# Late up-projections by a seven-product (Strassen-Winograd) scheme, weights' parts streamed from memory, in a kernel of windowed attention and two feed-forward nets

## The chip, the cores and the metric

The kernel runs on one core of a Trainium2 chip, in one launch. The metric is the device time in microseconds (us). The times below are of three runs and of one profiled execution.

## The reference

There are 4 sequences of 576 tokens (2304 tokens in all), 8 heads of 64, and a model width of 512. The weights arrive as 64-bit floats, q, k and v as 32-bit floats.

```python
scores = q @ k.T / sqrt(64) + alibi_bias        # causal, window of 128
x = softmax(scores) @ v                         # (2304, 512)
x = ((x @ w_a) * (x @ w_b)) @ w_out             # w_a, w_b (512, 1536), w_out (1536, 512)
h = x @ w_in                                    # (512, 2048)
g = where(h >= 1, h, where(h <= -1, 0, (h + 1) ** 2 / 4))
return g @ w_out2                               # (2048, 512)
```

## The kernel before, in words

Every matrix product of the two nets is made of three TensorE products, since each operand is kept as a rounded high part and the remainder as a low part: high by high, high by low, low by high. A weight matrix is cut into chunks of 128 hidden units: 12 chunks `a`, 12 `b` and 12 `o` for the first net, 16 `i` and 16 `p` for the second. `decode` turns one chunk of 64-bit words into its two parts, with operations on VectorE (DVE), ScalarE (ACT) and GpSimd (POOL), and `wp` holds 15 such pairs at a time.

An up-projection of one chunk (`up_steps`, lines 540 to 542) is 4 pieces of the model width by 3 products, 12 matmuls, into one PSUM bank of `mm`. In the first net `gate` multiplies the results of an `a` and a `b` chunk; in the second, `bend` applies the piecewise function. `parts` splits the result into `gh` and `gl` (line 562 and the helper `minus`, line 147, through which all such splits go). The down-projection of the chunk is another 12 matmuls, into the `acc` banks (`down1_half` line 613, `down1` lines 641 to 643, `down2` lines 679 to 681).

While the attention goes on, six half blocks of 256 tokens are passed through the first 4 or 5 chunks of the first net; their products stand between the attention's on TensorE. I call the stretch in which the attention and these half blocks are worked off the early part, and everything behind it the late part. There the tokens are taken in blocks of 512, 512, 512, 512 and 256. The hidden chunks are taken in groups (0 to 4, 4 or 5 to 8, 9 to 11 in the first net, 5, 6 and 5 chunks in the second); a group goes over all five blocks before the next begins, and so its weights stay. Between groups the sums of a block are kept in `xsum` or `osum`, and the new ones are added by VectorE. In the late part `mm` has four banks and `acc` four.

Each engine works off its own instructions in a fixed order, and so does the queue of SyncE (SP), which issues nearly all transfers. A scheduler wrote these orders when the program was built.

Of the kernel before, what the change touches and what calls it, by code (L numbers as in the profile page):

```python
# [9 lines left out]
F32 = mybir.dt.float32  # L10
# [16 lines left out]
def attention_and_two_ffns(  # L27
# [29 lines left out]
    blocks = [(t, min(TB, NT - t)) for t in range(0, NT, TB)]  # L57
# [3 lines left out]
    DEC = ['VVPP', 'VVPP', 'VVPP', 'AVPP', 'AVPP', 'AVPP', 'AVPP', 'AVPP', 'AVPP', 'AVPP', 'AVPP', 'AVPP', 'AVPP', 'AVPP', 'AVPP']  # L61
    DEC_LATER = 'AVVV'
    EB = 2
    EB2 = 2
# [6 lines left out]
    G2 = [5, 11]  # L71
# [8 lines left out]
    N0 = [4, 5, 5, 5, 5]  # L80
    N1 = 9
    NDIAG = 2
    NHALF = 6
    PACE = [0.8, 0.8, 0.5, 0.5, 0.5, 0.5, 0.5, 0.5, 0.3]
# [3 lines left out]
    TURN1 = [0, 1, 2, 3, 4]  # L88
    TURN2 = [4, 0, 1, 2, 3]
    UB = 1  # L90
    UB2 = 1
    VT = 3
    W2 = 2
    WARM = 0
    WB = 2
    WB2 = 2
    WP = 15
    HP = lambda n: n < HPN
    groups2 = [range(0, G2[0]), range(G2[0], G2[1]), range(G2[1], NF2)]
# [15 lines left out]
    if WARM:  # L115
        ps = ps_mm.tile([P, TB], F32, tag="mm", name="warm")
        for _ in range(WARM):
            nc.tensor.transpose(ps[:, :P], ident, ident)
# [21 lines left out]
    def x_tiles(i):  # L140
        n = blocks[i][1]
        return tuple(xp.tile([P, NC, n], F32R, tag=f"x{z}{i}", name=f"x{z}{i}") for z in "hl")

    xs = [x_tiles(i) for i in range(len(blocks))]
# [59 lines left out]
    def load_start():  # L204
        n = 0
        for nm in "qkv":
            start[nm] = []
            for i in range(NKB):
                start[nm].append(
                    wp.tile([P, H, D], F32, tag=f"w{'hl'[n % 2]}", name=f"{nm}{i}")  # L210
                )
                n += 1
            if TAIL < P:
                nc.gpsimd.memset(start[nm][-1][TAIL:], 0.0)
        if n % 2:
            wp.tile([P, H, D], F32, tag="wl", name="none")
        for z in range((n + 1) // 2):
            slots[0][2].append(("first", z))
# [145 lines left out]
    def values(b, hp, part):  # L364
# [31 lines left out]
        for z in range(2):  # L396
            mine = [m for m in ms if z < len(qblocks(m))]
            tok = lambda m: b * S + (2 * m + z) * D
            for i in sorted({tok(m) // TB for m in mine}):
                those = [m for m in mine if tok(m) // TB == i]  # L400
                c, n0 = (those[0] - ms[0]) * D, (tok(those[0]) - blocks[i][0]) // D
                src = po[z][:, c : c + len(those) * D].rearrange("p (n t) -> p n t", t=D)
                xh, xl = (
                    x[:, hp].rearrange("p (n t) -> p n t", t=D)[:, n0 : n0 + 2 * len(those) - 1 : 2]
                    for x in xs[i]
# [49 lines left out]
    order = [(z, f) for f in range(NF1) for z in "abo"] + [(z, f) for f in range(NF2) for z in "ip"]  # L455
    waiting = deque(order)
    wt = {}
    retired = {None}
    slots = [(wp, WP, deque())]
# [8 lines left out]
    def decode(key, pool):  # L468

        src = source(key)
        pool_, bw, be, bu = (later["dec"], WB2, EB2, UB2) if later else (wdec, WB, EB, UB)
        raw = pool_.tile([P, 4 * P], I64, tag="w64", name="w64", bufs=bw)
# [5 lines left out]
        wh = pool.tile([P, 4 * P], F32R, tag="wh", name="wh")  # L481
        wl = pool.tile([P, 4 * P], F32R, tag="wl", name="wl")
        e = pool_.tile([P, 4 * P], U32, tag="e", name="e", bufs=be)
        n = order.index(key)
        absolute, mult, add, less = DEC[n] if n < len(DEC) else DEC_LATER
        up = pool_.tile([P, 4 * P], U32, tag="up", name="up", bufs=bu)
        low = e.bitcast(F32)
        if absolute == "A":
            nc.scalar.activation(e.bitcast(F32), hi.bitcast(F32), AF.Abs)  # L489
        else:  # L490
            nc.vector.tensor_scalar(e, hi, 0x7FFFFFFF, None, ALU.bitwise_and)
        nc.vector.tensor_scalar(
            e.bitcast(F32), e.bitcast(F32), W64_MIN, W64_MAX, ALU.max, ALU.min
        )
# [15 lines left out]
    def pump():  # L510
        if not waiting:
            return False
# [291 lines left out]
```

## Time and profile before

| | |
|---|---|
| median of three runs | 996.48 us (995.35 to 998.64) |
| span of the profiled execution, first to last instruction | 994.4 us |
| TensorE (PE) busy | 969.7 us, 98% |
| weight loads (PEld) busy | 842.4 us, 85% |
| VectorE busy | 609.7 us, 61% |
| ScalarE busy | 407.2 us, 41% |
| GpSimd busy | 177.7 us, 18% |
| moved by DMA | 61.8 MB, mean 62 GB/s |

The profiled execution is 2.1 us shorter than the median of the runs, by its span. A TensorE instruction counts as busy until its result has come out of the array, and successive matmuls overlap; a busy share of 98% therefore doesn't say that the array takes a column in each cycle. How fast it goes is read from how many matmuls of one shape start in a stretch.

### The profile page before, as it was taken

Reading aid. Unit: us, or ns where it says so; the run is one execution under the profiler, and the core shown is the slowest. Engines: PE = TensorE matmul, PEld = TensorE weight load, DVE = VectorE, ACT = ScalarE, POOL = GpSimd, SP = SyncE. Lnnn points to the kernel's source line nnn. Section 1 sums busy time; section 2 is a strip of 40 time slices with the busy share of each in tenths; the row PEclk is TensorE's granted clock in tenths of the full one; section 3 lists DMA queues with packets and bytes.
Section 4 is the critical chain, followed back from the end, with each engine's and each line's share of the span. In section 5 each row is a group of like instructions: output and inputs, shape, how many; then the busy total and the mean of one; then the engine's idle time right before and its main releaser. Section 6 shows DMA issues by size and latency. Waiting matters only on the chain.

```text
span 994.4 us, 15931 instructions
## 1 busy us (share of the span) xinstructions
PE 969.7 (98%) x6052; PEld 842.4 (85%) x6052; DVE 609.7 (61%) x1366; ACT 407.2 (41%) x998; POOL 177.7 (18%) x285
## 2 busy tenths in 40 slices
PE   5997999999999999999999999999999999999998
PEld 4876999999989888888988888888888888888887
DVE  6699855553616993223995299635995446644443
ACT  5887677663214441112342245333552223322222
POOL 5567633331101100000212224000020000000001
PEclk9999999999999999999999999999999999999999
DMA  9756444213311331000331023100230000001111
GB/s 208 146 122 147 110 87 74 57 35 133 113 53 45 125 106 43 0 1 1 105 91 60 1 63 85 44 1 1 85 107 22 1 1 21 1 1 43 43 43 63
DMA packets 115403, 61.83 MB, mean 62 GB/s; under 512 B 87040, under 2 KB 107520, under 8 KB 114944
## 3 DMA queue, kind: packets, MB, share of 16 engines
q1 hardware_dynamic: 113184, 60.31, 22.7%
q8 instruction: 47, 0.77, 0.3%
q10 hardware_dynamic: 2144, 0.52, 0.2%
q14 instruction: 28, 0.23, 0.1%
HBM read 52.95 MB, written 7.86 MB: 61 GB/s over the span
## 4 chain that ended last, share of the span: by engine, by line
PE 87%; DVE 3%; DMA 1%; issue 1%; ACT 0%; POOL 0%; DVEq 0%; POOLq 0%; SPq 0%; ACTq 0%
PE mm L540 16%; PE mm L541 16%; PE mm L542 16%; PE acc L681 7%; PE acc L679 7%; PE acc L680 7%; PE acc L613 4%; PE acc L643 3%; PE acc L642 3%; PE acc L641 3%; PE ps_s L327 3%; PE ps_o L391 2%; PE ps_t L359 1%; DMA w<-in_moe_w_out_dram 1%; DVE e L499 0%
## 5 line engine op out<-in xcount | busy, mean ns | idle before, releaser
L540 PE MATMUL mm<-xh,wh 128*128 128x512 f32 (+1 forms) x912 | 318.6, 350 | 0.0
L541 PE MATMUL mm<-xl,wh 128*128 128x512 f32 (+1 forms) x912 | 315.6, 346 | 0.0
L542 PE MATMUL mm<-xh,wl 128*128 128x512 f32 (+1 forms) x912 | 315.0, 346 | 0.1
L540 PEld LDWEIGHTS mm<-xh,wh 128*128 128x128 f32 x912 | 173.0, 190 | 21.6
L541 PEld LDWEIGHTS mm<-xl,wh 128*128 128x128 f32 x912 | 173.1, 190 | 21.1
L542 PEld LDWEIGHTS mm<-xh,wl 128*128 128x128 f32 x912 | 172.8, 189 | 21.3 <-POOL wl L147 0.4
L596 ACT ACTIVATE c_sb<-c_sb,half 128x512 f32<-128x512 f32 (+1 forms) x80 | 54.5, 681 | 165.6 <-DVE c_sb L595 165.6
L585 DVE TENSOR_TENSOR a_sb<-mm,a_sb 128x256 f32<-128x256 f32 (+1 forms) x74 | 40.1, 542 | 121.1 <-PE mm L542 114.0
L679 PE MATMUL acc<-wh,gh 128*128 128x512 f32 x288 | 112.3, 390 | 0.2 <-ACT gh L562 0.2
L680 PE MATMUL acc<-wl,gh 128*128 128x512 f32 x288 | 112.2, 389 | 0.0
L681 PE MATMUL acc<-wh,gl 128*128 128x512 f32 x288 | 110.4, 390 | 0.3 <-POOL gl L147 0.3
L595 DVE TENSOR_SCALAR c_sb<-mm 128x512 f32<-128x512 f32 (+1 forms) x80 | 50.8, 636 | 81.9 <-PE mm L542 79.0
L147 POOL TENSOR_TENSOR gl<-c_sb,gh 128x256 fp32r<-128x256 f32 x16 | 15.6, 974 | 384.1 <-ACT gh L562 374.2
L147 POOL TENSOR_TENSOR gl<-a_sb,gh 128x256 fp32r<-128x256 f32 x40 | 35.4, 886 | 255.6 <-ACT gh L562 255.0
L597 DVE SCALAR_TENSOR_TENSOR c_sb<-mm,c_sb 128x512 f32<-128x512 f32 (+1 forms) x80 | 50.7, 635 | 39.0 <-ACT c_sb L596 39.0
L580 ACT COPY a_sb<-mm 128x256 f32<-128x256 f32 (+1 forms) x74 | 34.4, 464 | 89.2 <-PE mm L542 89.0
L562 ACT CAST gh<-a_sb 128x256 fp32r<-128x256 f32 (+1 forms) x74 | 37.2, 503 | 82.0 <-DVE a_sb L585 81.7
L562 ACT CAST gh<-c_sb 128x512 fp32r<-128x512 f32 (+1 forms) x80 | 46.2, 579 | 55.9 <-DVE c_sb L597 47.7
L506 ACT CAST wh<-e 128x512 fp32r<-128x512 f32 x68 | 42.2, 621 | 63.1 <-DVE e L505 38.2
L489 ACT ACTIVATE e<-w 128x512 f32<-128x512 f32 x65 | 43.8, 673 | 56.8 <-DVE wl L147 13.9
L642 PE MATMUL acc<-gl,wh 128*128 128x512 f32 (+1 forms) x184 | 66.3, 362 | 0.2 <-DVE gl L147 0.2
L337 ACT ACTIVATE s<-s,nmax 128x192 f32<-128x192 f32 (+2 forms) x144 | 62.0, 433 | 9.9 <-DVE nmax L333 9.5
(77 smaller groups left out, 1614.8 us busy)
## 6 DMA issues: line engine op xcount, KB each, us to landing
w<-in_moe_w_out_dram SPq DMA_DIRECT2D x28, 512.0 KB, 3.6
w<-in_moe_w_in_dram SPq DMA_DIRECT2D x16, 512.0 KB, 3.6
w<-in_moe_w_a_dram SPq DMA_DIRECT2D x12, 512.0 KB, 3.8
w<-in_moe_w_b_dram SPq DMA_DIRECT2D x12, 512.0 KB, 3.7
out_dram<-osum SPq DMA_DIRECT2D x18, 256.0 KB, 2.1
qraw<-in_q_dram SPq DMA_DIRECT2D x48, 72.0 KB, 2.8
kraw<-in_k_dram SPq DMA_DIRECT2D x48, 72.0 KB, 2.8
v<-in_v_dram SPq DMA_DIRECT2D x25, 128.0 KB, 2.8
```

The costliest lines, as they stand in the source:

```text
L147: eng.tensor_tensor(out_, a, hi.bitcast(F32), ALU.subtract)
L337: nc.scalar.activation(at(z, i), at(z, i), AF.Exp, bias=nmax[:, z : z + 1], scale=-1.0, accum_out=ssum[:, z : z + 1],)
L540: nc.tensor.matmul(ps, wh[:, cs], xh[:, c], start=(c == 0), stop=False)
L541: nc.tensor.matmul(ps, wh[:, cs], xl[:, c], start=False, stop=False)
L542: nc.tensor.matmul(ps, wl[:, cs], xh[:, c], start=False, stop=(c == NC - 1))
L562: nc.scalar.copy(hi[:, :n], t[:, :n])
L595: nc.vector.tensor_scalar(c_sb[:, :n], ph[:, :n], -1.0, None, ALU.max)
L596: nc.scalar.activation(c_sb[:, :n], c_sb[:, :n], AF.Square, bias=half, scale=0.5)
L642: nc.tensor.matmul(accs[c][:, :n], wh[:, cs], gl, start=False, stop=False)
L679: nc.tensor.matmul(accs[s], gh[:, ss], wh, start=begin, stop=False)
L680: nc.tensor.matmul(accs[s], gh[:, ss], wl, start=False, stop=False)
L681: nc.tensor.matmul(accs[s], gl[:, ss], wh, start=False, stop=end)
```

## The change

The early part keeps its form. The half blocks now pass through 4 chunks only, and the ScalarE, not GpSimd and VectorE, does a part of the decoding. While the attention goes on, 22 later chunks are decoded as well and stored to memory as 32-bit words (`early_job`).

In the late part the tokens are taken in three blocks of 768. The last block makes up the first 4 chunks in the old way (`gate_plain`), and then there are six visits: block 0, 1 and 2 through chunks 4 to 11 of the first net, then block 0, 1 and 2 through all 16 chunks of the second. A visit goes through all its chunks at once, so that its sums stay in six `acc` banks, and `mm` has the two banks that are left.

Two chunks of 128 hidden units (an `a` and its `b`, or two `i`) are projected up together. The model width is cut into halves of 256, the tokens into halves of 384, and the 2 by 2 by 2 block product is made of 7 products, not 8, each with 256 of the model width: 6 matmuls of 384 columns (`seven_steps`). What the seven products need is made beforehand: sums of weight blocks (`seven_job`) and of blocks of x (`x7_first`, `x7_second`), by VectorE and ScalarE. Counted from 0, the products q = 0, 2, 4 and 6 add up in one bank, q = 1 has the other, and q = 3 and 5 take it over; a bank is read after each product, before the next one adds to it.

The parts of the weights are made once, during the first visits, are stored to memory (`staged`), and are read from there into one of the 14 slots of `wp` for each later visit (`fill`). A list of down-projections that are still to do (`pieces`) is spread between the seven products (`after`). The order on TensorE is the written one in the late part (`manual_schedule`).

```diff
-    N0 = [4, 5, 5, 5, 5]
...
+    N0 = 4
...
-    WP = 15
+    WP = 14
+    GG = 2
...
+    EARLY = 22
...
+    HOLD = 3
...
+    BG = [(3, 2, 24), (3, 1, 24), (1.5, 1, 19), (2, 1, 12), (3, 1, 0), (3, 1, 0), (2, 1, 0)]
+    VISITS = [(1, 0), (1, 1), (1, 2), (2, 0), (2, 1), (2, 2)]
+    FLIP = [0, 1, 0, 0, 1, 0]
...
+    def words(key):
...
+        nc.scalar.activation(ef, hi.bitcast(F32), AF.Abs)
+        yield e, up
+        nc.scalar.activation(up, lo, AF.Copy, scale=2.0**-29)
+        yield e, up
+        nc.vector.tensor_scalar(ef, ef, W64_MIN, W64_MAX, ALU.max, ALU.min)
+        yield e, up
+        nc.vector.tensor_scalar(e, e, 5, 2, ALU.logical_shift_left, ALU.logical_shift_right)
+        yield e, up
+        nc.vector.scalar_tensor_tensor(e, hi, 0xC0000000, e, ALU.bitwise_and, ALU.bitwise_or)
+        yield e, up
+
+    def total_bits(dst, e, up):
+        shape = (lambda t: t.rearrange("p (a n) -> p a n", a=2)) if len(dst.shape) == 3 else (lambda t: t)
+        nc.vector.tensor_tensor(dst, shape(e), shape(up), ALU.add)
...
+    def early_job(key):
+        for e, up in words(key):
+            yield
+        total_bits(e, e, up)
+        early[key] = dram.tile([P, 4 * P], F32, name=f"w32_{key[0]}{key[1]}")
+        nc.sync.dma_start(early[key], e.bitcast(F32))
+        yield
...
+        t = w_tile("wb")
+        nc.scalar.copy(t[:, 0, :n], src)
+        yield
+        minus(V, t[:, 1, :n], src, t[:, 0, :n])
+        d = dram.tile([P, 2, n], F32, name=f"w_{key[0]}{key[1]}_{j}")
+        nc.sync.dma_start(d, t[:, :, :n].bitcast(F32))
...
+    def after(rate, nw, nx, most):
+        state["credit"] = min(state["credit"] + rate, 3.0)
+        while state["credit"] >= 1.0 and len(pieces) > HOLD:
+            state["credit"] -= 1.0
+            pieces.popleft()()
+        fill()
+        background(nw, nx, most)
...
+    def seven_steps(v, key, here):
+
+        ch = mm_bank()
+        z = None
+        for q in range(7):
+            if q in (1, 3):
+                z = mm_bank()
+            ps = z if q % 2 else ch
+            w = get(v, key, q // 2)
+            for ci in range(2):
+                cs = slice((q % 2) * 2 * P + ci * P, (q % 2) * 2 * P + (ci + 1) * P)
+                for n, (k, m) in enumerate(((0, 0), (0, 1), (1, 0))):
+                    nc.tensor.matmul(
+                        ps, w[:, k, cs], operand(here, q, ci, m), start=q in (0, 1, 3) and ci + n == 0,
+                        stop=ci == 1 and n == 2, skip_group_check=True,
+                    )
...
+    def gate7(v, f, here, hook):
+
+        s = {}
+        for q, ps in seven_steps(v, ("ab", f), here):
+            with urgent():
+                if q == 0:
+                    s[1] = st("s1")
+                    nc.scalar.copy(s[1], ps)
+                elif q == 1:
+                    a = work("a")
+                    plus(a[:, Q1], ps, s[1])
+                elif q == 2:
+                    s[2] = st("s2")
+                    nc.scalar.copy(s[2], ps)
+                elif q == 3:
+                    s[5] = st("s1")
+                    nc.scalar.copy(s[5], ps)
+                elif q == 4:
+                    plus(s[5], ps, s[5])
+                elif q == 5:
+                    plus(a[:, Q2], ps, s[2])
...
```

On TensorE, in the last group of the second net, a chunk's up-projection into one `mm` bank and then the down-projection of an earlier chunk stood like this before (`xh3` and `xl3` are the parts of block 3, `wh` and `wl` those of a chunk):

```order
L540 MATMUL mm_8825<-xh3_6899,wh_7085 128x512
L541 MATMUL mm_8825<-xl3_6900,wh_7085 128x512
L542 MATMUL mm_8825<-xh3_6899,wl_7086 128x512
L540 MATMUL mm_8825<-xh3_6899,wh_7085 128x512
L541 MATMUL mm_8825<-xl3_6900,wh_7085 128x512
L679 MATMUL acc_8794<-wh_6853,gh_8705 128x512
L680 MATMUL acc_8794<-wl_6854,gh_8705 128x512
L681 MATMUL acc_8794<-wh_6853,gl_8706 128x512
```

Now, in the second net's visits, products of 6 matmuls of 384 columns stand there (`ws` is a weight tile that came from memory, `xt` a sum of blocks of x, `z0` a plain piece of it), with one or two down pieces of 3 matmuls between them:

```order
L956 MATMUL mm_9675<-xt_7559,ws_9418 128x384 x6
L1138 MATMUL acc_9098<-ws_9341,gh_9508 128x512 x2
L1138 MATMUL acc_9098<-ws_9341,gl_9509 128x512
L1138 MATMUL acc_9099<-ws_9341,gh_9508 128x512 x2
L1138 MATMUL acc_9099<-ws_9341,gl_9509 128x512
L956 MATMUL mm_9619<-z0_7554,ws_9440 128x384 x3
L956 MATMUL mm_9619<-z1_7555,ws_9440 128x384 x3
L1138 MATMUL acc_9100<-ws_9341,gh_9508 128x512 x2
L1138 MATMUL acc_9100<-ws_9341,gl_9509 128x512
```

The shape went from 512 columns to 384, one `mm` bank is written again after one other product, and the weights of every product are new ones.

On SP's queue, in the late part, there were only loads of raw chunks (`w64`) before, one behind the other:

```order
L476 DMA w64_6815<-in_moe2_w_in_dram 128x4x128
L476 DMA w64_6851<-in_moe2_w_out_dram 128x512
L476 DMA w64_6913<-in_moe2_w_in_dram 128x4x128
L476 DMA w64_6957<-in_moe2_w_out_dram 128x512
L476 DMA w64_6999<-in_moe2_w_in_dram 128x4x128
```

Now, in the second visit (block 1, first net), loads of ready parts (`ws`) that wait for a slot, loads of raw chunks, and stores of new parts (`w_p0` from `wb`) that wait for VectorE share that queue:

```order
L489 DMA w64_6114<-in_moe2_w_in_dram 128x4x128
L921 DMA ws_5933<-w_ab7_3_4802 128x2x256
L703 DMA w_p0_0_5920<-wb_5907 128x1024
L921 DMA ws_5959<-w_o7_0_4839 128x1024
L921 DMA ws_5972<-w_ab6_0_4604 128x1024
L489 DMA w64_6335<-in_moe2_w_out_dram 128x512
L921 DMA ws_6009<-w_ab6_1_4609 128x1024
L921 DMA ws_6011<-w_ab6_2_4633 128x1024
```

The queue has 493 rows where it had 157, and a load now stands behind work of other engines.

On VectorE, in the fourth visit (block 0, second net), the reads of the `mm` banks (line 897) stand between the decoding of raw chunks (lines 501 to 510), the split of new weight parts (`wb`) and the chain of `bend` (line 999, and `gl`):

```order
L152 TENSOR_TENSOR wb_8008<-w32_7868,wb_8008 128x512
L897 TENSOR_TENSOR h0_7847<-mm_7902,s2_7886 128x384
L152 TENSOR_TENSOR wb_8013<-e_7897,wb_8013 128x256
L999 SCALAR_TENSOR_TENSOR c_7931<-h1_7927,c_7931 128x384
L501 TENSOR_SCALAR e_8110<-e_8110 128x512
L503 TENSOR_SCALAR e_8110<-e_8110 128x512
L152 TENSOR_TENSOR wb_8083<-e_8044,wb_8083 128x512
L505 SCALAR_TENSOR_TENSOR e_8110<-w64_8108,e_8110 128x512
L999 SCALAR_TENSOR_TENSOR c_7951<-h0_7847,c_7951 128x384
L510 ISA e_8110<-e_8110,up_8111 128x1024
L501 TENSOR_SCALAR e_8179<-e_8179 128x512
L897 TENSOR_TENSOR h0_8023<-mm_8016,s1_8000 128x384
```

Nothing of this stood there before in this form: the reads of `mm` were whole blocks of 512, and additions of weight blocks and of blocks of x were not made at all.

## Rows read from the trace of the kernel before

**Rows 1.** The page: busy time of each engine; bytes moved.

```profile
PE 969.7 (98%) x6052; PEld 842.4 (85%) x6052; DVE 609.7 (61%) x1366; ACT 407.2 (41%) x998; POOL 177.7 (18%) x285
DMA packets 115403, 61.83 MB, mean 62 GB/s; under 512 B 87040, under 2 KB 107520, under 8 KB 114944
```

**Rows 2.** Stretch, length; busy PE, PEld, DVE, ACT, POOL; clock; DMA share, GB/s.

```profile
0.00:100.00 100.00, 80.00 (x755) 69.22 (x756) 83.11 (x287) 75.05 (x255) 63.09 (x115) 0.94 0.75 156
100.00:235.00 135.00, 135.00 (x1561) 131.36 (x1561) 81.14 (x320) 89.74 (x323) 52.01 (x116) 0.99 0.31 67
700.00:750.00 50.00, 50.00 (x255) 42.75 (x255) 47.46 (x92) 24.67 (x44) 6.35 (x6) 1.00 0.27 85
850.00:900.00 50.00, 50.00 (x222) 41.39 (x221) 26.33 (x42) 12.76 (x20) 0.00 (x0) 1.00 0.01 3
570.00:605.00 35.00, 34.38 (x174) 28.85 (x173) 31.93 (x56) 17.55 (x31) 9.46 (x7) 1.00 0.21 60
```

**Rows 3.** Groups of TensorE instructions by line and shape, whole span.

```profile
L541 PE MATMUL mm<-xl,wh 128*128 128x512 f32 x528 | 205.5, 389 | 0.0
L679 PE MATMUL acc<-wh,gh 128*128 128x512 f32 x288 | 112.3, 390 | 0.2 <-ACT gh L562 0.2
L541 PE MATMUL mm<-xl,wh 128*128 128x256 f32 x384 | 110.1, 287 | 0.0
L642 PE MATMUL acc<-gl,wh 128*128 128x512 f32 x136 | 53.1, 390 | 0.2 <-DVE gl L147 0.2
L613 PE MATMUL acc<-gl,wh 128*128 128x256 f32 x112 | 31.9, 288 | 0.0
L642 PE MATMUL acc<-gl,wh 128*128 128x256 f32 x48 | 13.2, 283 | 0.0
```

**Rows 4.** Groups of TensorE by line and shape in the stretch 0 to 270.

```profile
L541 PE MATMUL mm<-xl,wh 128*128 128x256 f32 x224 | 64.9, 290 | 0.0
L613 PE MATMUL acc<-gl,wh 128*128 128x256 f32 x108 | 30.8, 288 | 0.0
L541 PE MATMUL mm<-xl,wh 128*128 128x512 f32 x8 | 3.1, 390 | 0.0
```

**Rows 5.** The chain that ended last, 240 to 272: start, length, merged instructions.

```profile
263.30 1.44 PE acc L613 x12
```

**Rows 6.** Timeline 245 to 248: start, length; weight load ahead of a matmul of 256 columns.

```profile
246.22 0.19 PEld L613 LDWEIGHTS acc<-gl,wh 128*128 128x128 f32 x1
```

**Rows 7.** Timeline of the end, TensorE and VectorE.

```profile
989.71 0.61 PE L681 MATMUL acc<-wh,gl 128*128 128x512 f32 x2
990.13 1.29 DVE L693 TENSOR_TENSOR osum<-acc,osum 128x512 f32<-128x512 f32 x2 [2.38 <-PE acc L681]
```

**Rows 8.** Timeline 712 to 726 (block of 256 tokens): TensorE's last matmul of a bank, VectorE.

```profile
715.65 0.28 PE L542 MATMUL mm<-xh,wl 128*128 128x256 f32 x1
...
716.07 0.69 DVE L147 TENSOR_TENSOR gl<-c_sb,gh 128x512 fp32r<-128x512 f32 x1
716.67 0.42 DVE L495 TENSOR_SCALAR e<-e 128x512 uint32<-128x512 uint32 x1
717.00 0.42 DVE L595 TENSOR_SCALAR c_sb<-mm 128x256 f32<-128x256 f32 x1
717.34 0.68 DVE L147 TENSOR_TENSOR wl<-e,wh 128x512 fp32r<-128x512 f32 x1
```

**Rows 9.** Groups of ScalarE by line and shape.

```profile
L489 ACT ACTIVATE e<-w 128x512 f32<-128x512 f32 x65 | 43.8, 673 | 56.8 <-DVE wl L147 13.9 <-DMA w<-in_moe_w_out_dram 12.2 <-DMA w<-in_moe_w_in_dram 10.7
L580 ACT COPY a_sb<-mm 128x512 f32<-128x512 f32 x34 | 19.8, 583 | 72.9 <-PE mm L542 72.9
L580 ACT COPY a_sb<-mm 128x256 f32<-128x256 f32 x40 | 14.5, 364 | 16.3 <-PE mm L542 16.2
```

**Rows 10.** DMA in 40 slices of 0.5 us, 230 to 250: busy tenths and GB/s.

```profile
DMA  0000000009389999999988999952100000004995
GB/s 0 0 0 0 0 0 0 0 0 180 82 328 410 442 410 442 410 410 426 442 291 299 356 340 354 375 186 88 45 8 0 0 16 0 0 0 156 356 86 131
```

More of the change, by code (lines that the diff above doesn't have):

```diff
@@ L526, in pump @@
+        with tc.high_priority() if HP(order.index(key)) else ExitStack():
+            decode(key)
         return True
@@ new lines, in run, with next_w, background @@
+    def run(jobs):
+        try:
+            return next(jobs[0]) != "no room"
+        except StopIteration:
+            jobs.popleft()
+            return True
+    def next_w():
+        if not jobs_w and late:
+            key = late.popleft()
+            jobs_w.append((seven_job if key[0] in ("ab", "ii") else plain_job)(key))
+        return bool(jobs_w)
+    def background(nw, nx, most):
+        state["bg"] = min(state.get("bg", 0.0) + nw, 8.0)
+        while state["bg"] >= 1.0:
+            state["bg"] -= 1.0
+            if not jobs_w and len(late) <= most:
+                break
+            if not next_w() or not run(jobs_w):
+                break
+        for _ in range(nx):
+            if not jobs_x:
+                break
+            run(jobs_x)
@@ new lines, in gate_plain @@
+    def gate_plain(b, f, hook):
+        a = work("a")
+        g = pair()
+        for n, (z, t_) in enumerate((z, t_) for t_ in (Q1, Q2) for z in "ab"):
+            ps = mm_bank()
+            w = wt[z, f]
+            for c in range(NC):
+                cs = slice(c * P, (c + 1) * P)
+                for k, (i, m) in enumerate(((0, 0), (0, 1), (1, 0))):
+                    nc.tensor.matmul(
+                        ps, w[:, i, cs], xs[b][c][:, m, t_], start=c + k == 0, stop=c == NC - 1 and k == 2
+                    )
+            with urgent():
+                if z == "a":
+                    nc.scalar.copy(a[:, t_], ps)
+                else:
+                    V.tensor_tensor(a[:, t_], ps, a[:, t_], ALU.mult)
+                    halves_of(g, t_, a[:, t_])
+            if t_ == Q2:
+                retired.add((z, f))
+            hook(n)
+        return [(f, g)]
@@ L769, in attention_and_two_ffns @@
                     pump()
+        if not later and begun >= 0:
+            for _ in range(XE):
+                if jobs_x:
+                    run(jobs_x)
+            if begun >= EFROM and ahead and not waiting and not jobs_w:
+                jobs_w.append(early_job(ahead.pop(0)))
+            for _ in range(WE):
+                if jobs_w:
+                    run(jobs_w)
         owed += PACE[min(begun, len(PACE) - 1)]
```

764 lines of the change are left out of this document (522 added, 242 removed).

## The prediction

> **What bounds the kernel now.** I read the page first: TensorE is busy 98% of the span, the other engines 61% and less [rows 1]. Busy counts matmuls that overlap, so I looked next at how often they start. In 850 to 900 us there is nothing but matmuls of 512 columns, 222 in 50 us at full clock [rows 2]: one in 225.2 ns. Twelve of 256 columns in a row take 1.44 us [rows 5]: one in 120 ns. The two give a line, 0.411 ns for a column and 14.8 ns for an instruction. By it a matmul of 384 columns would take 172.6 ns, and I use that.
>
> The groups of TensorE by shape [rows 3] give the late part's work. Each row stands for one of three like forms: 3 x (528 + 288 + 136) = 2856 matmuls of 512 columns and 3 x (384 + 112 + 48) = 1632 of 256. Of the latter 1008 belong to the six half blocks (28 passes through a chunk, 36 matmuls each). That leaves 2856 x 225.2 ns + 624 x 120 ns = 643.2 + 74.9 = 718.1 us for the late part. At 270 us, 3 x (224 + 108) = 996 of the 1008 and 24 of the late ones are done [rows 4]. So the early part would end at 270 - 5.4 + 1.4 = 266.0 us, with all else moved behind it. The last matmul starts at about 989.9 and its place ends at 990.2 [rows 7]: the late part takes 724.2 us, 6.1 more than its sum. The tail behind it, an addition and a store, is 4.2 us. The four terms are 266.0 + 718.1 + 6.1 + 4.2 = 994.4, the span.
>
> So TensorE's columns bound the late part. The other engines are there well below it, but for stretches: in 700 to 750 VectorE is busy 47.5 of 50 us, and TensorE still goes through [rows 2]. In 570 to 605, with VectorE at 31.9 of 35, TensorE shows 0.6 us of idle time; much of the 6.1 may lie there. The early part is another matter: in the first 100 us TensorE is idle for 20, with VectorE at 83; from 100 to 235 it has no idle time.
>
> **The change, part by part.** *TensorE, early.* 24 passes in place of 28: 144 matmuls of 256 columns less, 17.3 us. The attention's matmuls are the same.
>
> *TensorE, late.* Counted in the new order: the plain visit has 192 of 384 columns, 48 of 512 and 48 of 256. A pair of chunks in a visit to the first net has 42 of 384, 12 of 512 and 12 of 256 (11.39 us), and in the second net 42 of 384 and 36 of 512 (15.36 us). Each net has 8 pairs and 3 visits. Together 2208 of 384, 1200 of 512 and 336 of 256: 381.1 + 270.2 + 40.3 = 691.6 us. Of this 49.7 is the plain visit, 91.1 each of visits 1 to 3, 122.9 each of visits 4 to 6. Against 718.1 + 17.3, TensorE has 43.8 us less to do.
>
> The Trainium skill, "TensorE: Matmul & The Clock Gate", Back-to-back issue gap, gives N / 2.4 GHz + 2.5 ns between warm matmuls. The rows show 225.2 and 120 ns where it has 215.8 and 109.2. By it the saving would be 700.2 - 654.5 = 45.7 us; I keep to the rows.
>
> *Waits for the two banks.* A bank is read between two products that add to it. Tightest are q = 2 to 4 and 3 to 5 in the first net, read by ScalarE: between lie one product of another bank (1.036 us) and one down piece (3 x 225.2 ns = 0.676). From the start of the last matmul to the next use that is 0.173 + 1.036 + 0.676 = 1.885 us. Needed are the matmul itself (0.28 us for 256 columns [rows 8], 0.39 for 512 [rows 3], so 0.335), a wait in the reader's queue, and the read (364 to 583 ns [rows 9], so 0.475). VectorE's wait in the busiest stretch: the bank is full at 715.65 + 0.28 = 715.93 and is read from 717.00 [rows 8], 1.07 us. The sum is 1.88, just inside. So I take no stall there in general, and 8 us in all for the late part: somewhat more than the 6.1 now. Below, 2 us; above, see the rivals.
>
> *VectorE and ScalarE, late.* Back to back, VectorE takes 0.60 us for two operands of 512, 0.33 for one operand of 512 or for 256 columns [rows 8], so 0.465 for 384. Its fullest visit is the fourth: 106 instructions of 384, 39 of 512, 20 of 256, 6 of 768 (0.87), 28 single-operand ones and 14 of the new addition: 49.3 + 23.4 + 6.6 + 5.2 + 9.2 + 8.4 = 102 us in 122.9 (about 83%; the first visit: 77 of 91). ScalarE has 132 of 384 there at 0.475 and 58 others at 0.36 to 0.8 (0.673 for decoding [rows 9]): about 99 us. That is less than the 95% of VectorE which TensorE bore in 700 to 750. The new weights stand on VectorE's queue 12 us or more of TensorE's time ahead of their use. Cost nothing; without that cover it is the second rival.
> The addition of words (14 in that visit) goes by 1024 half words and no row shows it. The nearest row is an operation on 512 words, 0.60; if each half word counts as an element it is 1.2. I take 0.60, and would add 8 us to the fourth visit's VectorE at worst, which still fits.
>
> *The early decoding.* 22 chunks more, each two single-operand instructions, one of two operands and the addition on VectorE (0.33 + 0.33 + 0.60 + 0.60 = 1.86) and two on ScalarE (1.35): 41 and 30 us. From 100 to 235 us VectorE is busy 81 of 135 and ScalarE 90 [rows 2]. They would come to 122 and 120, about 90%. The attention's chains, through these same engines, run there too, so I take a cost of 4 us. Below: a gain of 10 (three chunks less are decoded for the first passes, where VectorE is fullest). Above: all 41.
>
> *Transfers.* By the sizes in the new order SP's queue carries 90 MB in visits 1 to 3 (273 us), 330 GB/s, where the whole kernel moved 61.8 MB [rows 1]. Wide transfers go at 410 to 442 GB/s in this trace [rows 10]. 14 slots of 2 us or so each are some 20 us of supply ahead. Cost nothing, with the cover gone a rival.
>
> The sum: 266.0 - 17.3 + 4 + 691.6 + 8 + 4.2 = 956.5, and with the 2.1 by which the median of the runs is above this execution, **958 us**.
>
> **The rivals.**
> *The early part is held by VectorE and ScalarE.* It speaks for it that they come to 90%, and that the first 100 us are already theirs. Against it: on average it fits. From +10 to +41 us: 968 to 995.
> *The late part is fed too slowly.* A raw chunk, a part to be stored and a part to be loaded stand one behind the other on SP, and VectorE stands still behind a chunk that is late, with the reads of the banks behind it. For it: the third visit has 34 MB in 91 us, 369 GB/s. Against it: rows 10's rates. If wide transfers went at 300 GB/s, 90 MB would take 300 us: +27. I give it +8 to +40: 966 to 998.
> The Trainium skill, "DMA: Bandwidth & Descriptors", Specifications, has about 358 GB/s of memory for a core. By that rule the third visit would need 94 us, 2.8 more than TensorE. The trace disagrees, with slices at 410 and more [rows 10].
> *The banks, the other side.* With two `mm` banks for four, each of 336 products waits for its bank to be read. A wait of 0.11 us for each product eats the remaining gain (38 us); at 0.25 us it is 84 less the 8 counted: about 1034. It speaks for it that 1.885 and 1.88 us are as good as equal, against it that 1.07 us was seen where VectorE was 95% busy.
> *A matmul of 384 columns is paced by its weights.* A weight load shows 0.19 us [rows 6], above 172.6 ns: 2208 x 17.4 ns = 38 us, no change (996). Against it: the same 0.19 us stands beside matmuls that start 120 ns apart.
>
> **How the numbers follow.** As summed 0.60 (945 to 970 us). Early part held 0.12; late part fed too slowly 0.13; banks, slower, 0.06; paced by weights 0.03; the early part shorter than summed 0.06 (938 to 945). A range from 940 to 985 holds the first, most of the second and third and half of the last: about 0.8. Runs of this kernel spread from 995.35 to 998.64, so a change within 0.3% (993.5 to 999.5) can't be told from none. Faster: 0.60 + 0.06 + nearly all of 0.12 and 0.13 = 0.89; same: 0.03 + a little of the two = 0.04; slower 0.07.
>
> **What would show it.** Right: stretches of the last two visits with a pair in about 15.4 us, rows of 384 columns 172 to 174 ns apart, the first matmul of the plain visit near 253 us, TensorE's idle time outside the first 100 us small. Wrong: TensorE waiting for VectorE or ScalarE reads of `mm` (banks); waiting for `ws` or VectorE for `w64` (feeding); the plain visit beginning after 265 us (early part); 384 columns at 190 ns.

## The result, and the profile after

| | before | after |
|---|---|---|
| median of the runs | 996.74 us (995.35 to 998.64, four) | 980.28 us (979.47 to 985.37, four) |
| span of the profiled execution | 994.4 us | 977.5 us |
| ratio of the times, 95% interval | | 0.985 (0.982 to 0.987) |

The kernel became faster by 16.5 us (1.5%), where I had forecast 38. The page of after, answering to [rows 1]: busy time of each engine, bytes.

```profile
PE 941.0 (96%) x6172; PEld 866.3 (89%) x6172; DVE 648.9 (66%) x1567; ACT 565.0 (58%) x1369; POOL 100.6 (10%) x215
DMA packets 172104, 212.45 MB, mean 217 GB/s; under 512 B 92400, under 2 KB 129776, under 8 KB 172016
```

The windows of after, with the columns of [rows 2]. The first two rows answer to the first two there; 307 to 590 are the three visits to the first net, and each of the last three is a visit to the second.

```profile
0.00:100.00 100.00, 84.43 (x762) 74.56 (x763) 75.42 (x263) 82.39 (x259) 48.65 (x99) 0.93 0.76 165
100.00:235.00 135.00, 123.36 (x1358) 116.41 (x1357) 102.93 (x374) 102.55 (x344) 46.15 (x106) 0.97 0.67 176
307.00:590.00 283.00, 279.81 (x1590) 264.13 (x1589) 212.08 (x427) 121.76 (x241) 0.00 (x0) 1.00 0.86 313
590.00:712.00 122.00, 121.50 (x616) 109.74 (x616) 106.45 (x213) 93.99 (x190) 0.00 (x0) 1.00 0.77 268
712.00:837.00 125.00, 125.00 (x624) 112.32 (x623) 55.25 (x102) 68.87 (x138) 0.00 (x0) 1.00 0.53 175
837.00:973.00 136.00, 136.00 (x672) 121.49 (x671) 53.34 (x98) 68.86 (x139) 0.00 (x0) 1.00 0.41 135
```

From 100 to 235 us TensorE is now idle for 11.6 us, where it had no idle time. In the visits to the second net it shows next to none, and yet each is longer than the sum for the matmuls that stand in it (616, 624 and 672 in these rows).

Groups of TensorE by shape, answering to [rows 3]: the counts are those of the new order, and most of the idle time shown lies in the early part (L555, L556).

```profile
L1138 PE MATMUL acc<-ws,gh 128*128 128x512 f32 x444 | 138.1, 392 | 0.0
L956 PE MATMUL mm<-xt,ws 128*128 128x384 f32 x612 | 123.4, 336 | 0.2 <-DVE a L897 0.2
L956 PE MATMUL mm<-z,ws 128*128 128x384 f32 x480 | 97.0, 337 | 0.5 <-DVE h L897 0.5
...
L556 PE MATMUL mm<-x,w 128*128 128x256 f32 x192 | 57.0, 298 | 1.4 <-DVE x L152 1.4
L555 PE MATMUL mm<-x,w 128*128 128x256 f32 x192 | 56.8, 301 | 1.5 <-ACT w L521 1.5
```

The timeline gives the two ends of the late part, the first matmul of the plain visit and the last of all:

```profile
260.83 2.35 PE L1046 MATMUL mm<-x,w 128*128 128x384 f32 x12 [0.92 <-ACT a_sb L579]
...
973.31 0.39 PE L1138 MATMUL acc<-ws,gl 128*128 128x512 f32 x1
```

Twelve matmuls of a half block (1.44 us) still stand behind the first row, so the early part, counted as in the prediction, ends at 262.3. The late part is 973.5 - 262.3 = 711.2, the tail 4.0. Set against the prediction's terms:

| term | forecast | measured |
|---|---|---|
| early part | 266.0 - 17.3 + 4 = 252.7 | 262.3 |
| sum of the late matmuls | 691.6 | 691.6 |
| late losses | 8 | 19.6 |
| tail | 4.2 | 4.0 |
| span | 956.5 | 977.5 |

So two terms are wrong, by 9.6 and 11.6 us. The late losses fall into three parts. The trace has every matmul of the late part, so I took the gap from each start to the next, and the gap that a shape settles to where it stands alone: 227 ns for 512 columns (thirty matmuls in the last rows of the kernel take 6.81 us), 173.2 for 384, 120 for 256. By these gaps instead of 225.2 and 172.6 the sum is 3.5 us longer. Gaps over these by more than 60 ns I call stalls: 7.8 us in all. The last 8.3 us are spread in small excesses over all visits, 1.8 to 1.9 us in each to the second net; I call this the spread excess. They can be read from the timeline of the last visit (start, length):

```profile
904.06 0.63 PE L1138 MATMUL acc<-ws,gh 128*128 128x512 f32 x2
904.52 0.40 PE L1138 MATMUL acc<-ws,gl 128*128 128x512 f32 x1
904.76 0.62 PE L1138 MATMUL acc<-ws,gh 128*128 128x512 f32 x2
905.22 0.40 PE L1138 MATMUL acc<-ws,gl 128*128 128x512 f32 x1
905.45 1.20 PE L956 MATMUL mm<-xt,ws 128*128 128x384 f32 x6
906.50 0.63 PE L1138 MATMUL acc<-ws,gh 128*128 128x512 f32 x2
```

Three matmuls of 512 take 0.70 us right behind a product of 384 (904.06 to 904.76), 0.69 behind another piece, where three by themselves take 0.68; a product takes 1.05 (905.45 to 906.50), not 1.04.

### The profile page after: what moved, and what is told of

It is laid out like the page before. It is cut to its first block, busy times and chain, and to the rows that moved or that the text cites. A ratio compares the mean times of both kernels' runs of the same rounds, so it can differ in the third digit from the quotient of the medians.

```text
span 977.5 us, 17546 instructions
## 1 busy us (share of the span) xinstructions
PE 941.0 (96%) x6172; PEld 866.3 (89%) x6172; DVE 648.9 (66%) x1567; ACT 565.0 (58%) x1369; POOL 100.6 (10%) x215
## 4 chain that ended last, share of the span: by engine, by line
PE 77%; DMA 8%; DVE 8%; ACT 4%; issue 2%; POOL 0%; SPq 0%; DVEq 0%; ACTq 0%; POOLq 0%
PE mm L956 32%; PE acc L1138 20%; PE acc L1077 10%; PE ps_s L330 3%; PE mm L1046 2%; PE ps_o L394 2%; DMA w<-in_moe_w_b_dram 2%; PE ps_t L362 1%; PE mm L557 1%; PE mm L556 1%; PE mm L555 1%; PE acc L604 1%; ACT s L340 1%; DMA xf<-xf 1%; DMA e<-w_b 1%
## 5 line engine op out<-in xcount | busy, mean ns | idle before, releaser
L1138 PE MATMUL acc<-ws,gh 128*128 128x512 f32 x444 | 138.1, 392 | 0.0
L956 PE MATMUL mm<-xt,ws 128*128 128x384 f32 x612 | 123.4, 336 | 0.2 <-DVE a L897 0.2
L956 PEld LDWEIGHTS mm<-xt,ws 128*128 128x128 f32 x612 | 107.4, 188 | 7.3 <-DVE a L897 0.8
L956 PE MATMUL mm<-z,ws 128*128 128x384 f32 x480 | 97.0, 337 | 0.5 <-DVE h L897 0.5
L956 PEld LDWEIGHTS mm<-z,ws 128*128 128x128 f32 x480 | 86.0, 188 | 7.6 <-DVE h L897 0.8
L1138 PEld LDWEIGHTS acc<-ws,gh 128*128 128x128 f32 x444 | 81.6, 188 | 9.3
L1138 PE MATMUL acc<-ws,gl 128*128 128x512 f32 x222 | 88.1, 397 | 0.0
L956 PE MATMUL mm<-x,ws 128*128 128x384 f32 x348 | 70.4, 336 | 0.6 <-ACT s L977 0.5
L1077 PE MATMUL acc<-gh,ws 128*128 128x512 f32 (+1 forms) x224 | 65.7, 337 | 0.0
L499 ACT ACTIVATE up<-w 128x512 uint32<-128x512 uint32 x68 | 45.7, 672 | 23.5 <-DVE e L510 14.2
L556 PE MATMUL mm<-x,w 128*128 128x256 f32 x192 | 57.0, 298 | 1.4 <-DVE x L152 1.4
L555 PE MATMUL mm<-x,w 128*128 128x256 f32 x192 | 56.8, 301 | 1.5 <-ACT w L521 1.5
```

The costliest lines, as they stand in the source:

```text
L499: nc.scalar.activation(up, lo, AF.Copy, scale=2.0**-29)
L555: nc.tensor.matmul(ps, w[:, 0, cs], xh[c], start=(c == 0), stop=False)
L556: nc.tensor.matmul(ps, w[:, 0, cs], xl[c], start=False, stop=False)
L956: nc.tensor.matmul(ps, w[:, k, cs], operand(here, q, ci, m), start=q in (0, 1, 3) and ci + n == 0, stop=ci == 1 and n == 2, skip_group_che ...
L1077: nc.tensor.matmul(dst, w[:, i, cs], m[:, t_], start=first and k == 0 and (n < NC or c % 2 == 0), stop=last and k == 2 and (n < NC or c % ...
L1138: nc.tensor.matmul(v["acc"][n], m[:, ss], w[:, i], start=first and k == 0, stop=last and k == 2,)
```

## The experiments

Each edit is one of after's code. "Plain visit" is the start of its first matmul. A stall is counted as above, from that matmul to the last. Both come from the one profiled execution; "(one)" marks a version that leaves work out and ran once. Since a scheduler writes the orders of the engines anew (in the early part TensorE's too), an edit in the early part also moves its neighbours. In e4, e14 and e8 the early part has after's order on every engine, and they began the plain visit at 258.8, 261.1 and 262.9 where after had 260.8: executions of one order differ by up to 4.1 us there, and a difference of that size in this column shows nothing. The profiled executions of e2, e3, e7 and e11 were 2.0 to 3.7 us longer than the median of their runs, and that of e16 was 2.9 us shorter.

| run | plain visit | late stalls | time, median |
|---|---|---|---|
| after | 260.8 | 7.8 | 980.3 |
| e1 no early decoding | 244.0 | 33.8 | 987.6 |
| e5 its instructions alone | 249.6 | 7.8 | 968.1 (one) |
| e6 its transfers alone | 269.4 | 10.3 | 990.3 (one) |
| e10 its loads, unread | 257.5 | 7.8 | 976.2 (one) |
| e2 three buffers | 264.6 | 8.7 | 980.4 |
| e3 load one ahead | 268.0 | 7.4 | 983.6 |
| e9 load three ahead | 256.9 | 10.5 | 978.8 |
| e11 and room for stores | 264.8 | 9.2 | 983.4 |
| e12 e9 without stores | 266.9 | 8.3 | 986.1 (one) |
| e7 spread | 271.8 | 9.6 | 988.6 |
| e16 begun later | 258.9 | 9.5 | 982.0 |
| e13 11 early | 254.4 | 30.0 | 995.6 |
| e15 11 early, e9, e14 | 248.6 | 33.1 | 991.7 |
| e14 five held back | 261.1 | 7.0 | 978.9 |
| e8 pieces in one batch | 262.9 | 33.0 | 1003.8 |
| e4 all of 384 columns, less work | 258.8 | 19.8 | 938.1 (one) |

### What the early decoding costs

**e1**, no early decoding.

```diff
-    EARLY = 22
+    EARLY = 0
```

> No chunk is decoded ahead while the attention goes on; all are decoded in the late part. If the 22 decodings are what holds the early part (theory: about 12 us, of which I had allowed 4), the first matmul of the plain visit moves from 260.8 to 247 to 251 us (266.2 less the 17.3 of the removed matmuls), and TensorE's idle time between 100 and 225 us falls from about 12 to under 3 us. Rival, the early part is longer for another reason (the decoder's new split between the engines, the loads of q and k): the plain visit still begins at 257 to 261. The late part takes over 41 us of VectorE's work in visits that have some 14 us of VectorE's time left each, so it should be longer than its 712 us by 5 to 40 us; whole time 975 to 1005.

The plain visit began at 244.0, earlier than I had put even the theory: the early part without these decodings ends at 244.0 + 1.4 = 245.4, which is 20.6 us less than before, not 17.3 (perhaps since fewer chunks are decoded in the first 100 us, the gain that I had only as a lower bound; no run separates it). Against the four executions of after's order the 22 decodings therefore cost 14.8 to 18.9 us. Done in the late part they cost more: 26 us of further stalls. By the spans (987.0 and 977.5) it still pays to do them early.

**e5** and **e6** take them apart. e5 reads one chunk over and over; e6 loads and stores, with one instruction on a single column in place of the six (two of ScalarE, four of VectorE; the seven in the expectation is a slip).

```diff
+        for e, up in words(key, same["raw"]):
...
+        if "d" in same:
+            early[key] = same["d"]
...
```

> The 22 early decodings keep all their instructions on VectorE and ScalarE, but read one raw chunk that was loaded once, and only the first result is stored: their 21 other loads and stores are left out (so the late part multiplies with other weights). Without any early decoding the plain visit began at 244.0 us, with all of it at 258.8 to 260.8. Theory that the amount of work on VectorE and ScalarE between the attention's links costs the 16 us: plain visit still at 256 to 261. Rival, the transfers (a raw chunk or a store that is late, ScalarE standing still behind it): plain visit at 244 to 249.

```diff
-        for e, up in words(key):
-            yield
-        total_bits(e, e, up)
...
+        nc.vector.tensor_scalar(
+            same[z][:, :1], raw[:, :1].bitcast(U32)[:, :1], 0, 0, ALU.bitwise_and, ALU.bitwise_and
+        )
```

> The reverse: the 22 early jobs load their raw chunks and store 22 tiles of zeros at the same places, and do no decoding; one instruction on a single column of VectorE takes the place of the seven (the late part multiplies by zeros there). Work theory: plain visit at 244 to 248 us. Transfer theory (the queue and the DMA engines are held up for the attention's own loads): 253 to 260. If waits of ScalarE for a raw chunk cost it, both this run and the one with the work alone are near 245, and only the two together give 260.

The windows 75 to 225 of e1, e5 and e6, in this order (columns as above):

```profile
75.00:225.00 150.00, 147.14 (x1699) 141.64 (x1700) 86.61 (x365) 106.69 (x384) 50.58 (x136) 0.98 0.32 65
```

```profile
75.00:225.00 150.00, 141.84 (x1571) 134.11 (x1571) 123.26 (x442) 124.00 (x407) 63.09 (x129) 1.00 0.33 67
```

```profile
75.00:225.00 150.00, 128.95 (x1407) 122.34 (x1407) 76.77 (x342) 90.81 (x335) 43.84 (x115) 0.94 0.69 177
```

The work theory falls. With all of the instructions VectorE and ScalarE are busy 123 and 124 of 150 us, and the plain visit is 5.6 us later than without (one execution each): the 4 us of the prediction were about right for that. With the transfers and hardly any work these two are the least busy of the three, and the early part is the longest, 25 us longer than in e1; its plain visit, at 269.4, is later than any theory of the expectation gave. The waits of e6 in the same stretch say who stands (engine, what it waits for: us in total, times, longest):

```profile
DVE zeros L663 <- DMA w<-in_moe_w_b_dram: 19.9, 6, 6.3
DVE zeros L663 <- DMA w<-in_moe_w_a_dram: 14.1, 7, 5.1
...
DVE zeros L663 <- DMA w<-in_moe_w_out_dram: 4.5, 4, 2.0
```

VectorE, which works off the attention in the same queue, stood 38.5 us behind raw chunks. In after it is ScalarE; its waits for them in 75 to 225 us:

```profile
ACT e L497 <- DMA w<-in_moe_w_out_dram: 3.8, 2, 3.0
ACT e L497 <- DMA w<-in_moe_w_a_dram: 3.4, 3, 1.5
ACT up L499 <- DMA w<-in_moe_w_out_dram: 1.8, 1, 1.8
ACT e L497 <- DMA w<-in_moe_w_b_dram: 1.0, 1, 1.0
```

The chain from 100 to 150 us shows what comes of it (start, length):

```profile
100.98 5.27 DMA w<-in_moe_w_a_dram
106.33 0.67 ACT e L497
...
107.37 0.42 DVE a_sb L582
...
117.35 5.14 DMA w<-in_moe_w_out_dram
122.58 0.67 ACT e L497
...
123.97 0.68 DVE diag L303
...
132.55 4.54 DMA w<-in_moe_w_b_dram
137.17 0.67 ACT e L497
```

Three times in 40 us the chain runs through a raw chunk of 4.5 to 5.3 us, then the decoding's first instruction, then the attention's work behind it. ScalarE's waits above are 10.0 us; in e1 and before it waits for no raw chunk.

**e10** was to show the loads with nobody behind them.

```diff
...
+        nc.vector.memset(raw[:, :1].bitcast(U32), 0)
+        yield
         nc.sync.dma_start(
...
```

> The 22 raw chunks are loaded at the places of the early decodings, and nothing reads them or waits for their landing except the next use of the buffer; there is no decoding and one store for the 22 (the late part multiplies by zeros there). In run e6 one instruction of VectorE stood behind each chunk, 35 us in all, and the plain visit began at 269. Theory of the engine that stands still: plain visit at 244 to 248. Rival, the transfers slow the attention's own loads: 254 to 268.

It didn't separate the two: VectorE's one-column instruction, which sets the pace, waited 29 us for the load that had the buffer before. What speaks against the rival is another reading: in none of the kernels does a list of waits for 75 to 225 show more than 0.8 us for a q, k or v.

### Attempts to get it back

**e2, e3, e9, e11, e12** give the transfers more room, step by step.

```diff
-    WB = 2
+    WB = 3
-    EB = 2
+    EB = 3
```

> Three buffers in place of two each for raw chunks and for words in the early part, no other change. If the early loss is ScalarE standing still in its queue behind a raw chunk or a store that is late (chain of after: 4.5 to 5.3 us each, several times), the slack of a third buffer takes most of it: plain visit from 252 to 256 us, time 970 to 976 us. If it is the mere amount of work on VectorE and ScalarE, nothing moves: plain visit 259 to 262, time 978 to 982.

```diff
...
+        if ahead:
+            fetch(ahead[0])
...
```

> The raw chunk of each early decoding is asked for one decoding ahead, and words have a third buffer. Theory of the late raw chunk: ScalarE no longer stands behind a load in 100 to 225 us, plain visit from 251 to 255 us, time 969 to 975. Rival, amount of work: plain visit 259 to 262, time 978 to 982.

```diff
...
+        for z in [key] + ahead[:3]:
+            if z not in raws:
+                fetch(z)
...
```

> All early decodings as they are, but their raw chunks are asked for three decodings ahead (two free slots of wp hold raw chunks beside the two of the old buffer), and words have a third buffer. Run e3 asked one ahead, and ScalarE still stood 25 us behind raw chunks, as each load stood on SP behind a store that waits for the decoding before it. Theory, a compute engine standing still behind a raw chunk that is late: ScalarE's waits for raw chunks in 95 to 215 us fall under 5 us, the plain visit begins at 249 to 253 us (249.6 with the work alone, run e5), the time is 966 to 972 us. Rival, the 17 MB themselves slow the attention's own loads: plain visit 257 to 265 us whatever ScalarE waits for, time 976 to 986.

> Run e9 with four buffers for words and two for y, so that neither ScalarE nor VectorE stands behind a store. In e9 the waits for raw chunks were gone, but the plain visit began at 256.9 us, 7 us behind the run with the work alone (249.6), and ScalarE still waited 7 us and VectorE 5 us for stores in 95 to 215. Theory, a compute engine that stands still behind a transfer: plain visit at 249 to 253, time 967 to 972. Rival, the loads and stores slow the attention's own loads of q and k: 255 to 259, time 974 to 980.

> Run e9 with the stores of 21 of the 22 early results left out (the late part multiplies with the first one's weights throughout). Theory, standing still behind a store: plain visit at 248 to 252. Rival, the 11.5 MB of raw loads slow the attention's own loads: still 254 to 258.

ScalarE's waits for raw chunks in 75 to 225 were 9.6 us in e2, 24.7 in e3, 3.3 in e9, 10.3 in e11 and 10.5 in e12. The longest goes with the latest plain visit and the shortest with the earliest of the five, but e2, e11 and e12 wait about as long as after and begin the plain visit 4 to 6 us later. ScalarE has a second wait for transfers, though: it stands behind the store of the words whose buffer it is to fill again. In e9 this is the longer one, in the same stretch:

```profile
ACT e L512 <- DMA w_o<-e: 2.7, 3, 1.6
...
ACT e L512 <- DMA w_a<-e: 2.2, 2, 1.7
ACT e L512 <- DMA w_b<-e: 2.1, 2, 1.6
```

So e9 took 6.7 us of waiting for raw chunks away and brought 5.5 us of waiting for stores (7.0, in after 1.5). Raw chunks and stores together make 9.5 us in e16 (below), 10.3 in e9, 11.5 in after (14.0, 15.4 and 18.4 in e4, e14 and e8, which have its order), 15.4 in e2, 16.5 in e11, 19.8 in e7 (below) and 24.7 in e3. With these sums e2 and e11 no longer stand out: by and large the plain visit begins later where ScalarE waits longer. That the two go together in single executions is no test, and e12, with 10.5 us and the plain visit at 266.9, doesn't fit. In e2, e9, e11 and e12 the decodings came to stand closer together (the first instruction of the last one is at 178, 172, 174 and 160 us, in after at 209), most of all in e12. Windows of e12:

```profile
120.00:130.00 10.00, 5.17 (x55) 3.84 (x57) 9.94 (x35) 8.98 (x28) 4.28 (x8) 0.88 0.95 260
130.00:140.00 10.00, 5.73 (x50) 4.45 (x47) 7.01 (x20) 4.20 (x11) 1.33 (x2) 0.67 0.91 213
140.00:150.00 10.00, 8.07 (x78) 6.53 (x80) 9.43 (x31) 9.17 (x31) 2.92 (x8) 0.67 0.64 202
```

TensorE idles for 4.8 us of the first ten, VectorE is full, and the granted clock of the next 20 us is 0.67. That is a mean of TensorE's two levels, 1.2 GHz for two thirds of the time and 2.4 GHz for the rest, and takes at most 20 x 0.33 = 6.6 us of full speed; less, as TensorE is busy for only 13.8 of the 20. In after the mean clock in 75 to 225 is 0.97, in e2, e11 and e12 0.93 to 0.94. The clock alone doesn't order the runs either: e3 had 0.98 and began the plain visit at 268.0.

**e7** and **e16** were to move decodings, **e13** and **e15** do half of them.

```diff
...
+            share += 0.75
+            if share >= 1.0:
+                share -= 1.0
...
```

> The 22 early jobs take a step at three of four places instead of at each, so that they reach to about 245 us, where the engines had free time, instead of 216. Work theory: fewer of them stand in each link of the attention, plain visit 255 to 259, time 974 to 979. Rival, each decoding costs the same wherever it stands (0.75 us): 259 to 262, no change.

```diff
-    EFROM = 1
+    EFROM = 2
```

> Run e9 with the early decodings begun one half block later, so that they stand beside the third to sixth half blocks and not beside the second (20 of them fit). In e9 TensorE lost 18 us between 75 and 150 us and nothing between 175 and 225, where fewer decodings stood. Theory, the place decides: plain visit at 248 to 253 us, late stalls 8 to 12 us, time 969 to 975. Rival, each decoding costs its 0.7 us wherever it stands: plain visit at 255 to 259, time 976 to 983.

```diff
-    EARLY = 22
+    EARLY = 11
```

> 11 chunks decoded early in place of 22. If the early part pays for each decoding alike (14.8 to 16.8 us for 22 by runs e1 and e4, 0.7 us each), the plain visit begins at 251 to 253 us; if it pays for where the decodings come to stand in the queues of ScalarE and VectorE, anywhere from 245 to 262. Late: the stalls of TensorE were 7.8 us with 22 and 33.8 with none, so 15 to 23 here; time 977 to 986, no gain over after.

> Raw chunks three ahead (run e9), 11 early decodings (e13) and five pieces held back (e14) together, to see whether a version is faster than after. If the three add up as the theories say: plain visit at 249 to 252, late part 713 to 722, time 970 to 978. If the place in the queues decides the early part: plain visit anywhere from 247 to 262.

e7 did spread them, to 235 us, and its plain visit was the latest of all: ScalarE waited 18.4 us for raw chunks. e16 (e9 with the edit shown) told nothing: the scheduler put its 20 decodings at 78 to 171 us, as in e9. With 11 early the plain visit moved by 6.4 us, about 0.6 for each; with 11, three ahead, it began at 248.6, 12.2 us earlier than after, with waits for raw chunks of 0.5 us. The late part took it all back: TensorE then waits 7.9 us in e13 for parts from memory (`ws`), and the stalls rise to 30 and 33 us, nearly those of e1. So the last eleven early decodings are worth more than the first: by the medians the first eleven lose 8.0 us (e13 against e1), and all 22 gain 7.3. No version that does all the work was measurably faster than after; e9 and e14 are 1.4 us below it, less than these runs can tell.

### The late part

**e4**, one shape for all matmuls of the second net.

```diff
-                    v["acc"][n], m[:, ss], w[:, i], start=first and k == 0, stop=last and k == 2,
+                    v["acc"][n][:, :QW], m[:, ss], w[:, i, :QW], start=first and k == 0, stop=last and k == 2,
```

> The second net's down-projection is made for 384 of its 512 output columns (the other 128 are left out), so that all matmuls of visits 4 to 6 have 384 columns. In the trace of after, three matmuls of 512 take 698 or 691 ns between products of 384 columns, and 680 ns where only 512 stand behind one another. Theory: the change of shape costs this, and then every matmul here starts 173.2 ns after the one before, and the fifth visit (624 of them) takes 107.7 to 108.4 us. Rival: it is the change of bank and of weights every 3 to 6 matmuls, and the same 18 and 11 ns for a piece and 6 to 22 ns for a product stay: 109.5 to 110.5 us.

The timeline of e4's last visit:

```profile
870.05 1.20 PE L956 MATMUL mm<-z,ws 128*128 128x384 f32 x6
871.09 0.51 PE L1138 MATMUL acc<-ws,gh 128*128 128x384 f32 x2
871.44 0.33 PE L1138 MATMUL acc<-ws,gl 128*128 128x384 f32 x1
871.61 0.51 PE L1138 MATMUL acc<-ws,gh 128*128 128x384 f32 x2
871.96 0.33 PE L1138 MATMUL acc<-ws,gl 128*128 128x384 f32 x1
872.13 1.20 PE L956 MATMUL mm<-z,ws 128*128 128x384 f32 x6
```

From 870.05 to 872.13 twelve matmuls take 2.08 us, 173.3 ns each, through three changes of bank. The spread excess of the last two visits fell from 1.9 to 0.1 us each: it is the change of shape. The fifth visit itself took 112.9 us, more than either theory had, as TensorE, with less to do, now had 4.7 us of stalls; without them it is 108.2, as the theory has it. Of these stalls and those of the fourth visit (9.4 us) the largest are waits for a y that is copied and for new parts (`wb`).

**e8**, all pieces of a pair behind its seventh product.

```diff
-        while state["credit"] >= 1.0 and len(pieces) > HOLD:
-            state["credit"] -= 1.0
+        state["n"] = state.get("n", -5) + 1
+        while state["n"] >= 0 and state["n"] % 7 == 0 and len(pieces) > HOLD:
             pieces.popleft()()
```

> The down pieces of a pair all stand behind its seventh product, none between the products. Shape changes fall to two in a pair: by run e4 the pace loss of visits 4 to 6 falls from 2.0 to 0.3 to 0.6 us each. Theory of the banks: the down pieces between the products are what hides the reads of the two mm banks. Without them 0.173 + 1.036 = 1.21 us are left from the start of a bank's last matmul to its next use, and the read needs 0.335 + 0.475 and its wait in the queue; a stall of 0.1 to 0.4 us at 5 places of each of 48 pairs is 24 to 96 us: 1000 to 1070 us. Rival, the banks come back in time by themselves: no stall, some 6 us faster than after, 972 to 976.

Both were right in part. The spread excess of the last two visits fell to 0.7 us, again with the changes of shape. The stalls rose from 7.8 to 33.0 us, on average about 0.1 for each of the 240 places of the expectation, and TensorE's waits are now for readers of the banks; the largest:

```profile
PE mm L956 <- DVE s L897: 3.8, 3, 2.3
PE mm L956 <- DVE a L989: 3.2, 7, 1.2
PE mm L956 <- ACT s L980: 1.9, 3, 1.0
```

They lie in the plain visit and the first four others: 31.4 us before 736 us, 1.6 behind. In the last two, where VectorE was busy for less than half of the time in after, 1.21 us are nearly always enough for a bank.

**e14**, pieces held back longer. TensorE's largest waits in after from 260 to 720 us:

```profile
PE acc L1077 <- DVE gl L152: 2.9, 3, 1.3
PE mm L1046 <- ACT a_sb L579: 0.9, 1, 0.9
PE mm L956 <- DVE h L897: 0.5, 1, 0.5
```

```diff
-    HOLD = 3
+    HOLD = 5
```

> Five down pieces are held back in place of three, so that a piece comes two products later behind the gl that it reads. In after, TensorE waits 1.0, 1.5 and 1.1 us for a gl of VectorE at 274, 338 and 514 us. Theory that these stalls of the late part are this one wait: they go, the late part is 3 to 4 us shorter (709 us from the first matmul of the plain visit to the last of all, where it was 712.5). Rival, VectorE is simply behind there and the next product waits for its bank instead: 712 to 713.

The same list of e14:

```profile
PE mm L956 <- DVE a L897: 3.1, 3, 1.3
PE acc L1077 <- DVE gl L152: 0.7, 1, 0.7
```

The rival holds: the late part is 711.9 us for 712.5. VectorE is behind at those places, and the wait moves from its `gl` to its read of the bank.

## Where the prediction was right, and the steps that failed

**The sum of the late part** was right but for 3.5 us: counts and gaps gave 691.6, and the gaps where a shape stands alone add 3.5 to that. One reading was off: the 222 matmuls in 850 to 900 us count one that began before 850; 221 begin there, and their starts lie 226.7 ns apart, not 225.2. So 512 columns took 227 ns before as well, some 5 of the 6.1 us that I read as losses before were this pace, and my 8 us were measured against losses that were not there: counted as above, the stalls before were 1.4 us. VectorE in the fourth visit was busy 106 of 122 us and ScalarE 94, forecast 102 and 99; back to back the addition of words took 0.60 us from start to start, as forecast. The rule of the Trainium skill, "TensorE: Matmul & The Clock Gate", Back-to-back issue gap, which that page gives for an isolated matmul and which gave a gain of 45.7 us, agrees in its slope and not in its constant: 227, 173.2 and 120 ns are N / 2.4 GHz plus 13.2 to 13.7 ns, where it has 2.5.

**Late losses, 8 us: mis-sized, 19.6 measured.** The line through the gaps was drawn from stretches of one shape each, and I used it for stretches in which 384 and 512 columns take turns. That is 8.3 us; e4 shows it for 5.1 of them, in the visits to the second net, and for the first net it is only argued from the same small excesses. The pace itself is 3.5. The stalls, 7.8 us, are what I had allowed, but 1.4 before; 2.9 of them are three waits for `gl`.

**Early part, 4 us for the early decoding: the step that failed.** I priced its instructions on VectorE and ScalarE, and these cost 5.6 (e5). In all the early decoding cost 16.9 in after (262.3 less the 245.4 of e1). The "Cost nothing" under *Transfers* was argued for the late part; the raw chunks and stores of the 22 early decodings were priced nowhere, though I had the queue of SP and the buffers in front of me. They are 17 MB (512 KB and 256 KB each), and with them the plain visit begins 9 to 13 us later than with the instructions alone (258.8 to 262.9 in the four executions of after's order, 249.6 in e5). How they do it is argued from after's chain and waits: ScalarE works off the attention and the decoding in one queue, and what stands behind a raw chunk that is late is the attention. Of the removed matmuls I had 17.3 us and got 20.6.

What stays open is how these 9 to 13 us divide. The trace shows 11.5 us of ScalarE's waits for raw chunks and stores of words in after, 5.0 us of VectorE's for stores of y (1.3 in e5), and a mean granted clock of 0.97 from 75 to 225 where e5 had 1.00 (150 x 0.03 = 4.5 us). The last two may not belong to the early decoding: e1, which has none, waited 4.3 us for stores of y and had a clock of 0.98. They overlap, and e9, e11 and e12, which were to take the waits away one by one, also changed the order, and e9 put one wait in place of another.

**The rivals.** The early part was late by about the smallest of what I had given the first rival (+10), but not by the amount of work on VectorE and ScalarE (e5). (Its bounds were not counted alike: 968 is the sum plus 10, and 995 is the sum plus 41 less the 4 in it.) My sign for it, a plain visit after 265 us, did not show, and yet the step had failed. The measured time lies between the 940 and 985 that I gave, with some luck: it is made of two losses, and no rival had either of them with its cause where it fell. That a compute engine stands still behind a late chunk was in my second rival, but for the late part. The late part was fed: 313 GB/s from 307 to 590 us, and no wait for `ws` among TensorE's in after. (In the late part ScalarE waited 5.1 us for raw chunks and VectorE 5.7 for early words; whether some of the stalls stand behind these, no run shows.) The Trainium skill, "DMA: Bandwidth & Descriptors", Specifications, has about 358 GB/s of memory for a core; the trace disagrees, as one of after's 40 slices of 24 us had 384. The banks held, by the down pieces between the products (e8). A matmul of 384 columns is not paced by its weights: 173.2 ns.

## What to carry to other kernels

Work that is put into idle time of an engine brings its transfers with it: price the wait at the head of each in-order queue that the new work enters, and who stands behind it, before the busy time. A gap between matmuls measured in a stretch of one shape holds for such a stretch; where shapes take turns, look for a row with the turns. And a cover that makes a tight wait free, as the down pieces do here, is found by taking it away: 25 us of stalls came out (e8).

## What the hardware showed that I had not expected

Turns between 384 and 512 columns cost 18 ns for a group of three behind a product, 11 for a second group, and 5 and more for a product of six, whatever the DMA did (the mean gap of 512 columns was 232 ns where it moved 313 GB/s and where it moved 135). Groups of six of 256 columns behind 384 took 0.71 us, less than the 0.72 of their own gap. And in e12, after 10 us in which TensorE had been idle for 4.8, the granted clock of the next 20 us was 0.67, two thirds of them at 1.2 GHz, so that a part of the stall was paid for a second time.
